# Attention and token mixer in one kernel: x transposed two column blocks ahead of the q products, v transposed one q tile later

## The chip, the cores and the metric

The kernel runs on one core of a Trainium2 chip. Its time is the device time of one execution in microseconds (us); the median of several executions is compared. The engines are TensorE (PE in the profile; PEld is its weight load), VectorE (DVE), ScalarE (ACT), GpSimd (POOL) and SyncE (SP), which issues most DMAs.

## What is computed

x is 2048 tokens by 640 channels. Attention has 32 heads of 20 channels, which share one k and one v; beside it stands a mixer that works across tokens; a gate per token blends the two.

```python
g = _sigmoid((x * gate_w).sum(-1, keepdims=True))
a = _A_ref(x, A_wq, A_wk, A_wv, A_wo)      # q = x@wq, k = x@wk, v = x@wv, softmax(q k^T * 20**-0.5) v, then @ wo
b = _B_ref(x, B_w1, B_b1, B_w2, B_b2)      # LayerNorm, then w1, gelu, w2 across the tokens
return g * a + (1 - g) * b
```

## The kernel before

All instructions are issued by hand in the order that the program writes (a manual schedule), and each engine works through its own list in that order. A step further back in one engine's list never passes an earlier one that waits.

The kernel has a first stage of about 97 us, which is the one that the change touches, and then the mixer's first product (w1), the attention with the rest of the mixer woven in, and a tail. The first stage makes q, k, v, the gate and the layer norm from x. It goes over four **token blocks** of 512 tokens (the loop over `sb`). Products are done in two parts, high and low, of x and of the weights: `wq_hi`, `wq_lo`, and for x the tiles `th`, `tl` (`slot` and `xT_hi`, `xT_lo` in the profile).

For a token block, x must be transposed first. `transpose_x(sb, cs)` transposes column blocks of 128 channels: four 128x128 transposes on TensorE (L292) per column block, into a PSUM bank from the pool `pst` (named `pt`, four banks) for column blocks 0 to 3, and from `psa` (named `pp`, four banks) for block 4. `split_x` then makes the high part on ScalarE (L285) and the low part on VectorE (L286).

The first token block is special, since all its data still has to arrive. SP issues, in turn, column block c of x (256 KB, L195) and rows c of the first three fifths of wq (192 KB, L197). `first_block` works by column block c: `turn(c)` casts wq's rows on GpSimd (`wq_hi`, L370), transposes x and splits it; `first_q(c, j, ahead)` does the products of the three q tiles `ahead` with part j of x (three products, L364); `wq_low` subtracts on GpSimd (L360). Before, the order on TensorE is: six products of a constant tile (L189), transposes of column block 0, two more products of the constant (L377), products 0 high, transposes 1, products 0 low, transposes 2, products 1, transposes 3, products 2, transposes 4, products 3, products 4. The constant products go to a bank that nothing reads.

Then every token block does the following. `project` makes k, v and the gate's logit in one product `pk` (L300, with `wkv_s`, whose low half GpSimd makes at L225); `split_kv` takes it out (L322 on ScalarE, L323 on VectorE, k_hi on ScalarE at L326, k_lo on GpSimd at L327). For each of the five q tiles `m`: transposes of the next token block (from `m` = 2 on: column blocks 0 and 1, then 2 and 3, then 4), the products of tile `m` (L300), `split_q` of the tile before (qh on ScalarE at L315, ql on VectorE at L316, two stores). `turn_v` transposes v and the gate's logit: it takes one bank of `pst`, does four small transposes on TensorE (L340) and two copies on VectorE, `v_sb` (L342) and `z_col` (L343). Between the tiles stand pieces of the layer norm, a generator `norm` that is moved on by `next`: statistics (L233, L234), a power on GpSimd (L242, between L241 and L244), the four small VectorE steps L244 to L247 that give `rstd`, the scaling `ht` (L252), and its split (L265 on ScalarE, L266 on GpSimd). In token block 0 the piece that follows q tile 0 holds L244 to L247, the first L252 and the first L265.

A tile from a pool takes the place of an earlier one, and its first writer waits until the readers of that one are done.

Of the kernel before, what the change touches and what calls it, by code (L numbers as in the profile page):

```python
# [17 lines left out]
P = 128  # L18
S, D, H, DH, F = 2048, 640, 32, 20, 1728
NS = S // P  # L20
DC = D // P
# [3 lines left out]
NB = 512  # L25
# [16 lines left out]
def mix_kernel(ctx: ExitStack, tc: tile.TileContext, A_x, A_wq, A_wk, A_wv, A_wo,  # L42
               B_x, B_w1, B_b1, B_w2, B_b2, gate_w, out):
    nc = tc.nc
# [17 lines left out]
    kst = const.tile([P, S], F32R, name="kst")  # L62
# [110 lines left out]
    with tc.tile_pool(name="pa", bufs=1) as pa, \  # L173
# [9 lines left out]
        def load_x(sb):  # L183
            for st in range(4 * sb, 4 * sb + 4):
                nc.sync.dma_start(out=xts[st], in_=x[st * P:(st + 1) * P, :])

        warm = psa.tile([P, NB], F32, name="pp")
# [32 lines left out]
        def split_wkv():  # L220
            for j in range(2):
                hi = wkv_s[:, :, 32 * j:32 * j + DH + j]
                lo = wkv_s[:, :, 64 + 32 * j:64 + 32 * j + DH + j]
                nc.scalar.activation(hi, wkv[:, :, j, :DH + j], AF.Copy)
                nc.gpsimd.tensor_sub(lo, wkv[:, :, j, :DH + j], f32(hi))  # L225
# [57 lines left out]
        def split_x(sb, c, pt):  # L283
            th, tl = x_tiles(sb, c)
            nc.scalar.activation(th, pt, AF.Copy)  # L285
            nc.vector.tensor_sub(tl, pt, f32(th))  # L286

        def transpose_x(sb, cs):
            pts = [(pst if c < 4 else psa).tile([P, NB], F32, name="pt" if c < 4 else "pp") for c in cs]
            for i in range(4):  # L290
                for c, pt in zip(cs, pts):
                    nc.tensor.transpose(pt[:, i * P:(i + 1) * P], xts[4 * sb + i][:, c * P:(c + 1) * P], ident)  # L292
            return [(sb, c, pt) for c, pt in zip(cs, pts)]

        def project(steps, pp=None, more=False):
            first = pp is None
            if first:
                pp = psa.tile([P, NB], F32, name="pp")
            for n, (w, t) in enumerate(steps):
                nc.tensor.matmul(pp, w, t, start=first and n == 0, stop=not more and n == len(steps) - 1)  # L300
            return pp

        def q_parts(m, ts):
            cols = slice(m * P, (m + 1) * P)
            return [[(wq_hi[:, c, cols], ts[c][0]) for c in range(DC)],
                    [(wq_hi[:, c, cols], ts[c][1]) for c in range(DC)],
                    [(wq_lo[:, c, cols], ts[c][0]) for c in (0, 3, 1, 4, 2)]]

        def split_q(sb, m, pp):
            if (sb, m) == (NQB - 1, DC - 1):  # L310
                qh, ql = (xin[0][:, i, :NB].bitcast(F32R) for i in range(2))
            else:
                qh = paw.tile([P, NB], F32R, name="qh")
                ql = paw.tile([P, NB], F32R, name="ql")
            nc.scalar.activation(qh, pp, AF.Copy)  # L315
            nc.vector.tensor_sub(ql, pp, f32(qh))  # L316
            for j, t in enumerate((qh, ql)):
                nc.sync.dma_start(out=q_scr[j, m * P:(m + 1) * P, sb * NB:(sb + 1) * NB], in_=f32(t))

        def split_kv(pp):  # L320
            kv = pa.tile([64, NB], F32, name="kv")
            nc.scalar.activation(kv, pp[64:, :], AF.Copy)  # L322
            nc.vector.tensor_add(kv, kv, pp[:64, :])  # L323
            k_hi = pa.tile([DH, NB], F32R, name="k_hi")
            k_lo = pa.tile([DH, NB], F32R, name="k_lo")
            nc.scalar.activation(k_hi, kv[:DH, :], AF.Copy)  # L326
            nc.gpsimd.tensor_sub(k_lo, kv[:DH, :], f32(k_hi))  # L327
            return kv, k_hi, k_lo

        def store_k(sb, k_hi, k_lo):  # L330
            cols = slice(sb * NB, (sb + 1) * NB)
            for b in range(2):
                for j, t in enumerate((k_hi, k_hi, k_lo)):
                    o = 64 * b + DH * j
                    nc.sync.dma_start(out=f32(kst[o:o + DH, cols]), in_=f32(t))
# [23 lines left out]
        def wq_low(c, cols, raw):  # L359
            nc.gpsimd.tensor_sub(wq_lo[:, c, cols], raw, f32(wq_hi[:, c, cols]))  # L360

        def first_q(c, j, ahead):
            for m, pp in enumerate(ahead):
                nc.tensor.matmul(pp, wq_hi[:, c, m * P:(m + 1) * P], xT[0, c][j], start=c == 0 and j == 0, stop=False)  # L364

        def first_block():
            ahead = [psa.tile([P, NB], F32, name="pp") for _ in range(QW // P)]

            def turn(c):
                nc.gpsimd.tensor_copy(wq_hi[:, c, :QW], wqs[c])  # L370
                split_x(*transpose_x(0, (c,))[0])

            turn(0)
            for c in range(DC):
                if c == 0:
                    for i in range(2):
                        nc.tensor.matmul(warm, kst[:, :P], kst[:, :NB], start=True, stop=True)  # L377
                    first_q(c, 0, ahead)
                if c + 1 < DC:
                    turn(c + 1)  # L380
                for j in range(c == 0, 2):
                    first_q(c, j, ahead)
                wq_low(c, slice(0, QW), wqs[c])
            load_x(1)
            split_wkv()
            for c in range(DC):
                nc.scalar.activation(wq_hi[:, c, QW:], wqs2[c], AF.Copy)
            for c in (0, 3, 1, 4, 2):
                wq_low(c, slice(QW, D), wqs2[c])
            norm = layer_norm(0)  # L390
            for _ in range(3):
                next(norm)
            return ahead, norm

        due = None
        for sb in range(NQB):
            ahead, norm = first_block() if sb == 0 else ([], layer_norm(sb))
            ts = [xT[sb, c] for c in range(DC)]
            pk = project([(wkv_s[:, c, :], t) for c in range(DC) for t in ts[c]])
            if due:  # L400
                split_q(*due)
            kv, k_hi, k_lo = split_kv(pk)
            if 0 < sb < NQB - 1:
                load_x(sb + 1)
            store_k(sb, k_hi, k_lo)
            if sb:
                next(norm)
            for m in range(DC):
                turned = []
                if sb + 1 < NQB and m > 1 and (sb, m) != (2, DC - 1):  # L410
                    turned = transpose_x(sb + 1, ((0, 1), (2, 3), (4,))[m - 2])
                p = q_parts(m, ts)
                if m < len(ahead):
                    pp = project(p[2], ahead[m])
                elif m < DC - 1:
                    pp = project(p[0] + p[1] + p[2])
                else:
                    pp = project([p[r][c] for c in range(DC) for r in range(3)])
                if m:
                    split_q(*due)  # L420
                due = sb, m, pp
                if m == 0:
                    turn_v(sb, kv)
                for t in turned:
                    split_x(*t)
                if sb == 1 and m == 1:
                    turn_bias()
                if sb == 1 and m == 0:
                    w1_load(3)
                if sb == 2 and 0 < m < 4:  # L430
                    w1_upto(m)
                if sb == 3 and m == 1:
                    w1_upto(4)
                    new_qmax(0)
                if sb == 3 and m == 3:
                    gates()
                for _ in range(1 + (sb and m > 1 or sb == 3)):
                    next(norm, None)
            if sb == 2:
                for t in transpose_x(3, (4,)):  # L440
                    split_x(*t)
# [92 lines left out]
    chain, ahead = [], []  # L534
# [68 lines left out]
    with tc.tile_pool(name="psl", bufs=4, space=PSUM) as psl, \  # L603
# [9 lines left out]
        for fc in range(PRO):  # L613
            pu = [psb.tile([P, NB], F32, name=f"pu{r}") for r in range(2)]
            for hf in range(4):
# [4 lines left out]
                for c in range(HS):  # L620
                    st = hf * HS + c
                    for k, (w, h) in enumerate(((wh, h_hi[0]), (wh, h_lo[0]), (wl, h_hi[0]))):
                        for r in range(2):
                            rows = slice(64 * r, 64 * r + 64)
                            nc.tensor.matmul(pu[r][:, :HD2], w[rows, c, :], h[rows, st, :],  # L625
                                             start=(st == 0 and k == 0), stop=(st == NS - 1 and k == 2))
# [410 lines left out]
    m = len(ph)  # L1037
# [213 lines left out]
    def turn(a, cut):  # L1251
        blocks, cols = slice(a * NB // 64, (a + 1) * NB // 64), slice(a * NB // 2, (a + 1) * NB // 2)
        flat = ot[:, blocks].rearrange("p c e -> p (c e)")
        nc.vector.transpose(flat, o[:, cols])
        nc.vector.reciprocal(rl[:, blocks], ot[:, blocks, DH])
        if cut is not None:
            low(cut)
        nc.vector.tensor_mul(ot[:, blocks], ot[:, blocks], rl[:, blocks, None].to_broadcast([P, NB // 64, 32]))
        nc.vector.transpose(on[:, cols], flat)
        nc.scalar.activation(oh[:, cols], on[:, cols], AF.Copy)  # L1260
# [61 lines left out]
```

## Time and profile before

| | us |
|---|---|
| median of 3 runs | 1618.52 (1618.24 to 1618.57) |
| profiled execution | 1618.09 |
| its span, first to last instruction | 1616.3 |
| TensorE busy in the span | 1609.4 |
| VectorE, ScalarE, GpSimd busy | 1353.7, 1309.0, 868.7 |

A row of the profile's timeline gives the start and the duration in us, the engine, the line of the kernel, the operation, what it writes and reads, the shapes and how often; in square brackets is the idle time of the engine before it and what ended that. Rows that are alike and follow each other are merged. A row of the list of waits gives who waited for whom: us in total, times, the longest. Matmuls overlap in the pipeline, so the distance from one start to the next tells what one costs TensorE.

### The profile page before, as it was taken

The page shows a single profiled execution, that of the slowest core. Times are in us where ns is not written, and L with a number is a line of the kernel's source. Part 1 is how long each engine was busy: PE and PEld are TensorE (multiplying, and loading weights), DVE is VectorE, ACT ScalarE, POOL GpSimd, SP SyncE. Part 2 cuts the span into 40 slices and gives each one's busy share as a digit, 9 for nine tenths or more (in the row PEclk, how much of TensorE's full clock was granted, in tenths as well). Part 3 has the DMA queues.
Part 4 walks back from the last instruction along what each step waited for, and adds up shares of the span by engine and source line. Part 5 has one row for each costly group of instructions (what it writes and reads, how often), then busy time and mean ns, then how long its engine had stood idle before and what let it go on. Part 6 is the DMA issues. An engine that isn't in the chain of part 4 may idle for free.

```text
span 1616.3 us, 39559 instructions
## 1 busy us (share of the span) xinstructions
PE 1609.4 (100%) x14877; PEld 1125.7 (70%) x14877; DVE 1353.7 (84%) x2344; ACT 1309.0 (81%) x2567; POOL 868.7 (54%) x974
## 2 busy tenths in 40 slices
PE   9999999999999999999999999999999999999999
PEld 7889677777777777666666666666666666666666
DVE  6689999999999999888888888888888888666643
ACT  4545788888888888888888888888888888999975
POOL 6568667786777687644544444454544443344410
PEclk9999999999999999999999999999999999999999
DMA  7655223323332232222222221222222212336521
GB/s 216 211 162 150 72 69 79 87 69 93 81 85 71 82 83 65 65 73 81 72 69 73 54 72 55 66 73 81 73 73 69 68 46 70 94 107 192 160 69 45
DMA packets 188245, 144.51 MB, mean 89 GB/s; under 512 B 43473, under 2 KB 150126, under 8 KB 188054
## 3 DMA queue, kind: packets, MB, share of 16 engines
q1 hardware_dynamic: 187766, 141.66, 31.4%
q8 instruction: 117, 1.92, 0.5%
q14 instruction: 74, 0.61, 0.1%
q10 hardware_dynamic: 288, 0.33, 0.1%
HBM read 108.38 MB, written 32.15 MB: 87 GB/s over the span
## 4 chain that ended last, share of the span: by engine, by line
PE 98%; SPq 1%; DVE 0%; ACT 0%; DMA 0%; issue 0%; DVEq 0%; ACTq 0%
PE ms L739 16%; PE g L817 11%; PE s L739 10%; PE ms L704 10%; PE g L1005 9%; PE s L704 8%; PE s L492 6%; PE ms L492 6%; PE pp L300 4%; PE o L739 4%; PE pu L625 3%; PE o L704 3%; PE o L492 2%; PE g L950 2%; PE s L905 1%; PE ml L492 1%
## 5 line engine op out<-in xcount | busy, mean ns | idle before, releaser
L498 DVE TENSOR_REDUCE mp<-s 128x1 f32<-128x512 f32 x878 | 576.8, 681 | 54.5 <-PE s L492 46.2
L713 ACT ACTIVATE p<-ms 128x512 f32<-128x512 f32 x935 | 544.2, 615 | 49.5 <-PE s L739 16.3
L498 DVE TENSOR_REDUCE mp<-ms 128x1 f32<-128x512 f32 x775 | 511.5, 681 | 78.8 <-PE ms L492 64.8
L713 ACT ACTIVATE p<-s 128x512 f32<-128x512 f32 x833 | 488.1, 617 | 34.1 <-PE ms L739 10.7
L752 POOL TENSOR_TENSOR acc<-acc,part 128x512 f32<-128x512 f32 x212 | 274.5, 1295 | 443.2 <-ACT part L751 425.7
L704 PE MATMUL ms<-qst,kst 62*128 62x512 f32 x935 | 366.4, 408 | 0.1
L492 PE MATMUL s<-kst,qmx 60*128 60x512 f32 x878 | 350.8, 414 | 0.6 <-DVE yo L548 0.5
L704 PE MATMUL s<-qst,kst 62*128 62x512 f32 x833 | 323.9, 409 | 0.2 <-ACT p L713 0.2
L492 PE MATMUL ms<-kst,qmx 60*128 60x512 f32 x775 | 307.4, 411 | 0.0
L1005 PE MATMUL g<-slot,wh 64*128 64x320 f32 x1344 | 305.9, 312 | 0.0
L739 PE MATMUL ms<-p,v_sb 128*32 128x512 f32 x2208 | 265.5, 598 | 0.0
L1005 PEld LDWEIGHTS g<-slot,wh 64*128 64x128 f32 x1344 | 216.6, 184 | 68.7 <-issue 55.3
L498 DVE TENSOR_REDUCE mp<-o 128x1 f32<-128x512 f32 x301 | 205.2, 682 | 47.2 <-PE o L492 40.6
L131 POOL TENSOR_TENSOR wl<-wr,wh 128x512 fp32r<-128x512 f32 (+1 forms) x176 | 218.0, 1238 | 29.4 <-ACT wh L128 12.5
L704 PEld LDWEIGHTS ms<-qst,kst 62*128 62x128 f32 x935 | 171.0, 185 | 63.1 <-ACT p L713 23.9
L1005 PE MATMUL g<-slot,wl 64*128 64x320 f32 x672 | 205.2, 305 | 0.0
L817 PE MATMUL g<-slot,wh 64*128 64x320 f32 x864 | 196.3, 309 | 0.0
L817 PE MATMUL g<-u,wh 64*128 64x320 f32 x864 | 196.3, 309 | 0.0
L704 PEld LDWEIGHTS s<-qst,kst 62*128 62x128 f32 x833 | 153.2, 185 | 45.9 <-ACT p L713 29.8
L713 ACT ACTIVATE p<-o 128x512 f32<-128x512 f32 x267 | 164.5, 616 | 11.1 <-PE ms L739 5.5
L739 PE MATMUL s<-p,v_sb 128*32 128x512 f32 x1392 | 167.4, 598 | 0.2 <-ACT p L713 0.2
L492 PEld LDWEIGHTS s<-kst,qmx 60*128 60x128 f32 x878 | 161.4, 185 | 5.0 <-DVE yo L548 0.7
(243 smaller groups left out, 3093.7 us busy)
## 6 DMA issues: line engine op xcount, KB each, us to landing
wr<-in_B_w_dram SPq DMA_DIRECT2D x136, 256.0 KB
qmx<-q_scr SPq DMA_DIRECT2D x192, 80.0 KB
qst<-q_scr SPq DMA_DIRECT2D x192, 80.0 KB
ot<-l_scr SPq DMA_DIRECT2D x120, 64.0 KB
y_scr<-yo SPq DMA_DIRECT2D x16, 320.0 KB
slot<-o_scr SPq DMA_DIRECT2D x16, 320.0 KB
o_scr<-ot SPq DMA_DIRECT2D x124, 40.0 KB
o_scr<-acc SPq DMA_DIRECT2D x124, 40.0 KB
```

Of the source, the lines that this page charges most:

```text
L131: nc.gpsimd.tensor_sub(wl[:, :nv], wr[:, :nv], f32(wh[:, :nv]))
L300: nc.tensor.matmul(pp, w, t, start=first and n == 0, stop=not more and n == len(steps) - 1)
L492: nc.tensor.matmul(ms, qmax[n][64 * b:64 * b + 60, pr, qt * P:(qt + 1) * P], kst[64 * b:64 * b + 60, kq * NB:(kq + 1) * NB], start=True, s ...
L498: r = nc.vector.tensor_reduce(mtiles[n][:, c, kq:kq + 1], ms, axis=AX.X, op=ALU.max)
L625: nc.tensor.matmul(pu[r][:, :HD2], w[rows, c, :], h[rows, st, :], start=(st == 0 and k == 0), stop=(st == NS - 1 and k == 2))
L704: nc.tensor.matmul(s, kst[64 * b:64 * b + 62, kb * P:(kb + 1) * P], q[64 * b:64 * b + 62, pr, :], start=True, stop=True)
L713: e = nc.scalar.activation(p, s, AF.Exp, scale=SCALE)
L739: nc.tensor.matmul(o[32 * hh:32 * hh + 32, :], v_sb[:, kb + i, :], ptiles.pop((u, hh)), start=opened and i == 0, stop=(i == len(us) - 1) a ...
L752: nc.gpsimd.tensor_add(sums[0], sums[0], part)
L817: other_tile(half, nc.tensor.matmul(hold["p"][:, :HD2], w[r, i, :], u[d][r, fc, :], start=(hold["n"] == 1), stop=(hold["n"] == 6 * FC - 3)))
L950: other_tile(half, nc.tensor.matmul(hold["p"][:, :HD2], o[r, c, :], w[r, c, d * HD2:(d + 1) * HD2], start=(hold["n"] == 1), stop=(hold["n" ...
L1005: other_tile(half, nc.tensor.matmul(hold["p"][:, :HD2], w[r, st % HS, :], h[d][r, st, :], start=(hold["n"] == 1), stop=(hold["n"] == 6 * NS)))
```

## The change

In the first token block column block 1 is turned (cast, transposed, split) before the first products, and in the loop column block c + 2 instead of c + 1. The two constant products are gone. In every token block `turn_v` is called after the products of q tile 1 instead of those of q tile 0, so its transposes stand on TensorE behind tile 1's products, and its copies stand on VectorE behind the ql of tile 0.

```diff
             turn(0)
+            turn(1)
+            first_q(0, 0, ahead)
             for c in range(DC):
-                if c == 0:
-                    for i in range(2):
-                        nc.tensor.matmul(warm, kst[:, :P], kst[:, :NB], start=True, stop=True)
-                    first_q(c, 0, ahead)
-                if c + 1 < DC:
-                    turn(c + 1)
+                if c + 2 < DC:
+                    turn(c + 2)
                 for j in range(c == 0, 2):
                     first_q(c, j, ahead)
                 wq_low(c, slice(0, QW), wqs[c])
...
-                if m == 0:
+                if m == 1:
                     turn_v(sb, kv)
```

## The prediction

> **What bounds the kernel now.** I read the chain of waits on the page first, then TensorE's waits, then the first 42 us engine by engine, because the diff touches nothing later: with buffer numbers left out, every engine's order after the four token blocks is the same in both programs.
>
> ```profile
> span 1616.3 us, 39559 instructions
> ...
> PE 98%; SPq 1%; DVE 0%; ACT 0%; DMA 0%; issue 0%; DVEq 0%; ACTq 0%
> ```
>
> TensorE holds 98% of the chain that ended last, so a stretch in which it stands still early is added to the end one for one. All its recorded waits together are small; these two lie in the code that is changed:
>
> ```profile
> PE pp L364 <- ACT slot L285: 0.3, 1, 0.3
> PE pt L340 <- DVE kv L323: 0.2, 1, 0.2
> ```
>
> So there is at most half a microsecond to win at these two places, and the question is what the new order makes TensorE wait for. Its own rows in time (start, duration, engine, line, what, count):
>
> ```profile
> 1.43 2.93 PE L189 MATMUL pp<-kst 128*128 128x512 f32 x6 [1.43 <-DVE kst L68]
> 4.16 1.05 PE L292 MATMUL pt<-ident,xa 128*128 128x128 f32 x4
> 4.87 0.82 PE L377 MATMUL pp<-kst 128*128 128x512 f32 x2
> 5.99 0.94 PE L364 MATMUL pp<-slot,wq_hi 128*128 128x512 f32 x3 [0.31 <-ACT slot L285]
> 6.78 0.60 PE L292 MATMUL pt<-ident,xa 128*128 128x128 f32 x4
> 7.13 0.96 PE L364 MATMUL pp<-slot,wq_hi 128*128 128x512 f32 x3
> ...
> 14.09 0.86 PE L364 MATMUL pp<-xT_lo,wq_hi 128*128 128x512 f32 x3
> 14.78 2.03 PE L300 MATMUL pp<-slot,wkv_s 128*128 128x512 f32 x8
> ...
> 22.34 1.03 PE L292 MATMUL pt<-ident,xb 128*128 128x128 f32 x8
> 23.14 1.17 PE L300 MATMUL pp<-slot,wq_hi 128*128 128x512 f32 x4
> ```
>
> Four transposes of a column block take 0.35 us of TensorE (6.78 to 7.13), three q products 0.79 after a pause (5.99 to 6.78) and 0.69 in a run (14.09 to 14.78, 0.23 each), eight transposes 0.80 (22.34 to 23.14). The k/v product starts at 14.78.
>
> **Part 1: transposes of x two blocks ahead.** They read x column block c+1, and whether it has landed is told by the queue. x and wq blocks alternate on SP's queue, and GpSimd waits for wq's:
>
> ```profile
> 6.96 0.51 POOL L370 CAST wq_hi<-xb 128x384 fp32r<-128x384 f32 x1 [2.26 <-DMA xb<-in_A_wq_dram]
> 7.43 1.03 POOL L360 TENSOR_TENSOR wq_lo<-xb,wq_hi 128x384 fp32r<-128x384 f32 x1
> 8.44 0.50 POOL L370 CAST wq_hi<-xb 128x384 fp32r<-128x384 f32 x1
> ...
> 13.73 0.76 POOL L225 TENSOR_TENSOR wkv_s<-wkv,wkv_s 128x100 fp32r<-128x100 f32 x2
> 14.43 3.54 POOL L360 TENSOR_TENSOR wq_lo<-wr,wq_hi 128x256 fp32r<-128x256 f32 x5
> 18.08 1.04 POOL L242 TENSOR_TENSOR r<-ve,mhalf 128x4 f32<-128x4 f32 x1
> 19.37 1.28 POOL L327 TENSOR_TENSOR k_lo<-kv,k_hi 20x512 fp32r<-20x512 f32 x1 [0.24 <-ACT k_hi L326]
> ```
>
> wq block 1 lands at 6.96. Sizes, and the rate in these microseconds (the last column is GB/s):
>
> ```profile
> xa<-in_A_x_dram SPq DMA_DIRECT2D x5, 256.0 KB
> xb<-in_A_wq_dram SPq DMA_DIRECT2D x4, 192.0 KB
> ```
> ```profile
> 6.00:7.00 1.00, 1.00 (x6) 0.81 (x7) 0.57 (x1) 0.00 (x0) 0.04 (x1) 1.00 1.04 326
> 7.00:8.00 1.00, 1.00 (x8) 0.81 (x7) 0.00 (x0) 0.59 (x1) 1.00 (x2) 1.00 0.94 303
> 8.00:9.00 1.00, 1.00 (x8) 0.92 (x7) 0.69 (x1) 0.45 (x2) 1.00 (x3) 1.00 1.12 368
> ```
>
> The DMA engines are saturated (share 0.94 to 1.12), so landings follow the bytes. Estimates from these rows: x block 1 came 192 KB before wq block 1, at 326 GB/s 0.60 us, so at 6.4; x block 2 behind it at 6.96 + 262/303 = 7.8; wq block 2 at 7.8 + 197/303 = 8.45, which agrees with the cast at 8.44; x block 3 at 8.45 + 262/368 = 9.2.
>
> Now the new order. On TensorE the transposes of block 1 stand in front of the first q products. Those ran from 5.99, in the very time in which block 1 was still on its way; now they wait behind it to 6.4 + 0.35 = 6.75. Next: products to 7.55, transposes of block 2 from 7.8 (waiting) to 8.2, low products to 9.0, transposes of block 3 from 9.2 (waiting) to 9.55. By then twelve transposes (blocks 1 to 3) and six products are done; the old order had done the same twelve and twelve products by about 10.05 (7.13 + 0.79 + 0.35 + 6 x 0.23 + 0.35). Six more products are 1.4, so it stands at 10.95 where it stood at 10.05: **0.9 us late**.
>
> GpSimd is late too, by itself. turn(c) puts the cast of wq block c ahead of the low part of the block before. The old order computed the low part of block 0 (7.43 to 8.44) while block 2 of wq was arriving; the new one waits for block 2, casts it at 8.44, and the low part comes after. GpSimd is busy without a gap from there, so everything behind shifts by one low part, 1.0 us: the low half of wkv_s ends at 15.5 instead of 14.49, the power at L242 runs from 19.0 to 20.05. The k/v product needs wkv_s, so both roads put it at about 15.6, **0.8 late**. The two constant products removed (4.87 to 5.69) stood in idle time: nothing gained, since TensorE is idle to 6.4 now. SP's queue keeps its order, and the one load that waits for GpSimd's low parts, load_x(1), stays where it is:
>
> ```profile
> 14.25 1.77 SPq L185 DMA_DIRECT2D xb<-in_A_x_dram  x4
> ```
>
> The low parts of blocks 0 to 3 that it needs end one part later than before, at about 13.7, still ahead of this issue.
>
> **Part 2: the transposes of v one q tile later.** The step turn_v holds four transposes on TensorE and two copies on VectorE, no DMA. In block 0 the transposes no longer wait for kv. But the copies move on VectorE's queue too, behind ql of q tile 0:
>
> ```profile
> 19.21 0.24 DVE L342 COPY v_sb<-pt 128x80 f32<-128x80 f32 x1 [0.58 <-POOL r L242]
> 19.36 0.15 DVE L343 COPY z_col<-pt 128x4 f32<-128x4 f32 x1
> 19.43 1.24 DVE L244 TENSOR_TENSOR r<-r 128x4 f32<-128x4 f32 x1
> ...
> 21.31 1.13 DVE L252 TENSOR_SCALAR ht<-xa,mv,rstd 128x640 f32<-128x640 f32 x2
> 23.44 0.69 DVE L316 TENSOR_TENSOR ql<-pp,qh 128x512 fp32r<-128x512 f32 x1 [1.00 <-ACT qh L315]
> ```
>
> And somebody waits for them: v's four transposes take one of the four pst banks, and at q tile 3 the second of the two transpose tiles (x blocks 2 and 3, TensorE at 22.34) takes the same bank; in the built program its first transpose waits for the z_col copy. Copies at 19.5 were no obstacle. Copies behind ql, which ends at 24.13, are one: that ql is late because ACT's queue holds the layer norm's casts ahead of qh, and these wait for ht at 21.31, the end of the rstd steps L244 to L247.
>
> When does this chain run in the new kernel? L244 took 1.24 us beside k_lo on GpSimd (19.37 to 20.65) and ended with it: one of them waits for the other. [...] The same happens again: the power ends at 20.05, k_lo starts 4.6 to 4.8 us after the k/v product did (19.37 - 14.78), at 20.3, and holds to 21.6; the rstd steps need 0.6 to 0.8 and are caught. ht then starts at 21.9 to 22.2, I take 22.1, 0.8 later than before; ql ends at 24.13 + 0.8 = 24.9; the copies end 0.3 later (19.21 to 19.51), 25.25; the transposes go on at 25.3, with seven of eight left (0.7), and q tile 3's products start at 26.0 instead of 23.14: **2.9 us late**. TensorE itself would be there at 22.34 + 0.8 - 0.2 (the wait for kv, gone) = 22.95, so 2.3 of it is a new wait, and it swallows the 0.8 of part 1 and the gain on kv. What queues behind the waiting transpose is all of TensorE; VectorE's ql of tile 1, 0.3 us of copies later than otherwise, frees a bank that is wanted at tile 4, fifteen products (3.5 us) after tile 3 begins, and costs nothing.
>
> In blocks 1 to 3 the bank that v takes is not wanted until long after the copies; there the move only puts v's transposes beside others:
>
> ```profile
> 36.19 0.39 PE L300 MATMUL pp<-slot,wq_lo 128*128 128x512 f32 x1
> 36.51 0.42 PE L340 MATMUL pt<-ident,kv 21*128 21x21 f32 x4
> 36.86 1.20 PE L300 MATMUL pp<-slot,wq_hi 128*128 128x512 f32 x4
> ```
>
> Four of them take 0.35 (36.51 to 36.86), and the change of kind costs 0.1 before (36.19 + 0.23 to 36.51) and about 0.1 after. One pair of changes goes in block 1, about one change in block 2, none in block 3: -0.25, bounds 0 and -0.5.
>
> **Sum.** +2.9 - 0.25 = **+2.65 us**, +0.16%. Against the profiled execution (1618.09 us, span 1616.3) that is 1620.75; it lies 0.4 under the median of 1618.52, so the prediction is **1621.2**. A measurement of this kernel can tell about 0.2%, 3.24 us, from no change: the forecast is a loss just inside it. Each of the eight terms is read to 0.1 or 0.2, so the sum is good to about 0.6, and the bound is one such step away.
>
> **Rivals.**
> *The rstd steps escape.* If k_lo starts 0.6 us later against the power than I have it (at 20.9), all four steps are done before it, ht starts at 20.9, and the copies end at 24.0: products at 24.8, +1.7 - 0.25 = +1.4, 1619.9. A TensorE later in part 1 than reckoned does that. Against it: both shift by nearly the same. 0.10, within the bound.
> *No new wait at tile 3.* If the bank is free by 22.95, part 1 and the gains nearly cancel, 0.8 - 0.2 - 0.25 = +0.35, 1618.9; and if x block 1 is there when the first transposes end (4.87), part 1 goes as well and 0.45 us is won: the change then does what its order suggests, and still within the bound. Against it: ql ended at 24.13 even before. 0.09.
> *The copies are held.* They ran while GpSimd was idle; now they run beside its subtractions, and may be held as L244 was, up to 1.1 each: +0.9 to +1.8 more, 1622.1 to 1623.0. Against it: ql at 23.44 has the same source kind (PSUM) and took 0.69. [...] 0.09.
> *TensorE stays slow* (slower side, clear). The first constant products go one in 0.45 us (1.43 to 4.16 for six), later ones in 0.23, while the profile's column of the granted clock says 1.00 throughout: TensorE starts at half speed and is released by 5.99. Two products of the busy stretch before that go, and TensorE idles from 4.87 to 6.4. If the release slips by a few microseconds, the wait at tile 3 hides it, since that wait is set by GpSimd and VectorE; it decides from about 15 us on, and half speed from there to 20 us would add 2.5 more, 1623.7. [...] 0.06.
>
> **How the numbers follow.** My case has 0.64, of which 0.18 lies above the bound (over 3.24) and 0.46 within. Slower by over 0.2%: 0.18 + 0.09 (held copies) + 0.06 (slow TensorE) = 0.33. Within: 0.46 + 0.10 (escape) + 0.09 (no wait) = 0.65. No case gives a gain over the bound; 0.02 is left for something after the four blocks that I don't see. The range leaves out the case without a wait (0.09), that 0.02 and a long slow start (0.06): from 1619.4, under the escape, to 1623.0, the held copies.
>
> **What would show it.** In the profile after: TensorE's second transposes (L292) at about 6.4 and the first q products after, at 6.75; a gap before the casts of wq block 2 on POOL; wkv product near 15.6; L342 and L343 right after the first L316; a wait of about 2.3 us of TensorE on L343 at 22.9, and tile 3's products at 26. Wrong if the L292 pair at tile 3 runs without waiting, if the first products still start at 6.0, or if the change goes past 100 us.

## The result and the profile after

| | before | after |
|---|---|---|
| median, us | 1618.24 (22 runs, 1617.83 to 1618.82) | 1621.15 (22 runs, 1619.57 to 1622.13) |
| profiled execution, us | 1618.09 | 1620.42 |
| its span, us | 1616.3 | 1618.6 |

The ratio is 1.0017, with an interval of 1.0012 to 1.0023: 2.9 us slower, just inside the 0.2% that the prediction took for the bound of what can be told apart; the interval reaches a little beyond it. The times of after spread over 2.6 us, those of before over 1.0.

The engines in the chain that ended last, from the page of after:

```profile
PE 99%; ACT 0%; DVE 0%; DMA 0%; issue 0%; SPq 0%; DVEq 0%; ACTq 0%
```

TensorE still carries the whole chain, so what it loses early arrives at the end. Its waits in the changed code (us in total, times, longest):

```profile
PE pt L292 <- DVE z_col L343: 1.3, 1, 1.3
PE pt L292 <- DMA xa<-in_A_x_dram: 1.0, 1, 1.0
```

Neither is in the list of before. The first is the bank of v at q tile 3, the second x column block 1, which is still on its way. The timeline of TensorE in after:

```profile
6.17 1.12 PE L292 MATMUL pt<-ident,xa 128*128 128x128 f32 x4 [0.96 <-DMA xa<-in_A_x_dram]
6.94 1.63 PE L364 MATMUL pp<-slot,wq_hi 128*128 128x512 f32 x3
8.37 1.05 PE L292 MATMUL pt<-ident,xa 128*128 128x128 f32 x4
9.07 1.41 PE L364 MATMUL pp<-slot,wq_hi 128*128 128x512 f32 x3
10.32 0.60 PE L292 MATMUL pt<-ident,xa 128*128 128x128 f32 x4
...
16.74 2.03 PE L300 MATMUL pp<-slot,wkv_s 128*128 128x512 f32 x8
...
23.92 0.27 PE L292 MATMUL pt<-ident,xb 128*128 128x128 f32 x1
25.51 0.95 PE L292 MATMUL pt<-ident,xb 128*128 128x128 f32 x7 [1.32 <-DVE z_col L343]
26.22 1.17 PE L300 MATMUL pp<-slot,wq_hi 128*128 128x512 f32 x4
```

Three products took 1.43 us (6.94 to 8.37) and then 1.25 (9.07 to 10.32), 0.48 and 0.42 each, where before had 0.26: in this execution TensorE came off its half speed only at 10.1 (10.11 on the clock's record). So the k/v product is 1.96 late (16.74 against 14.78). At q tile 3 one transpose of eight goes through at 23.92 and the next waits for the bank; tile 3's products are 3.08 late (26.22 against 23.14). GpSimd and VectorE in the same execution:

```profile
8.32 0.51 POOL L370 CAST wq_hi<-xb 128x384 fp32r<-128x384 f32 x1 [1.15 <-DMA xb<-in_A_wq_dram]
...
18.96 1.04 POOL L242 TENSOR_TENSOR r<-ve,mhalf 128x4 f32<-128x4 f32 x1
21.33 1.26 POOL L327 TENSOR_TENSOR k_lo<-kv,k_hi 20x512 fp32r<-20x512 f32 x1 [1.32 <-ACT k_hi L326]
23.52 5.28 POOL L266 TENSOR_TENSOR slot<-ht,slot 128x320 fp32r<-128x320 f32 x6 [0.94 <-ACT slot L265]
```
```profile
19.91 0.68 DVE L323 TENSOR_TENSOR kv<-kv,pp 64x512 f32<-64x512 f32 x1 [1.02 <-ACT kv L322]
20.51 0.15 DVE L244 TENSOR_TENSOR r<-r 128x4 f32<-128x4 f32 x1
...
21.29 2.17 DVE L252 TENSOR_SCALAR ht<-xa,mv,rstd 128x640 f32<-128x640 f32 x2
24.46 0.69 DVE L316 TENSOR_TENSOR ql<-pp,qh 128x512 fp32r<-128x512 f32 x1 [1.00 <-ACT qh L315]
25.07 0.23 DVE L342 COPY v_sb<-pt 128x80 f32<-128x80 f32 x1
25.22 0.15 DVE L343 COPY z_col<-pt 128x4 f32<-128x4 f32 x1
```

GpSimd waits for wq block 2 (1.15) before the cast at 8.32, and its power at L242 is 0.9 later than before. On VectorE the copies stand right behind ql, and the waiting transpose starts 0.14 after the second has ended. The mixer's first product starts 2.59 late (98.81 against 96.22), so the later token blocks gave back 0.49 of the 3.08. From there to the end the shift falls by 0.2 more.

### The profile page after: what moved, and what is told of

Its sections match the earlier page's. It is cut to its first block, busy times and chain, and to the rows that moved or that the text cites. A ratio compares the mean times of both kernels' runs of the same rounds, so it can differ in the third digit from the quotient of the medians.

```text
span 1618.6 us, 39555 instructions
## 1 busy us (share of the span) xinstructions
PE 1610.1 (99%) x14875; PEld 1126.9 (70%) x14875; DVE 1352.4 (84%) x2344; ACT 1308.7 (81%) x2567; POOL 869.0 (54%) x974
## 4 chain that ended last, share of the span: by engine, by line
PE 99%; ACT 0%; DVE 0%; DMA 0%; issue 0%; SPq 0%; DVEq 0%; ACTq 0%
PE ms L737 16%; PE g L815 11%; PE s L737 10%; PE ms L702 10%; PE g L1003 9%; PE s L702 8%; PE s L490 6%; PE ms L490 6%; PE pp L300 4%; PE o L737 4%; PE pu L623 3%; PE o L702 3%; PE o L490 2%; PE g L948 2%; PE s L903 1%; PE ml L490 1%
```

## Experiments

Each kernel was run in turns with before (medians 1618.37 us in the first set, 1618.44 in the second and third).

**The two parts alone.** `e1_v_only` is before with only the move of v's transposes:

```diff
-                if m == 0:
+                if m == 1:
                     turn_v(sb, kv)
```

> Only part 2 of the change: turn_v after q tile 1, the first block as before. Theory A (the wait of q tile 3's transposes on v's copies sets the loss): k_lo runs at 19.4 as before and holds the layer norm's chain to 20.65, ql of tile 0 ends near 23.5, the copies at 23.85, TensorE arrives at 21.9 and waits 2.0 us; products of tile 3 at 24.6 against 23.14, less 0.5 saved in later blocks: +1.0 us, 1619.2. Theory B (the loss is the late first block alone, v's move is harmless): the kv wait and the later savings are won, -0.5 to -0.9, 1617.5.

Measured: 1619.55 (11 runs), ratio 1.0009 (1.0000 to 1.0018), +1.2, near theory A. Nine runs lie from 1619.32 to 1619.80, two at 1620.95 and 1621.09. TensorE in its profile:

```profile
24.34 0.95 PE L292 MATMUL pt<-ident,xb 128*128 128x128 f32 x7 [1.63 <-DVE z_col L343]
```

The wait for the bank is there with the first block's x order as before, so it belongs to part 2 alone.

`e2_x_only` is after with `turn_v` back at `m == 0`:

```diff
-                if m == 1:
+                if m == 0:
                     turn_v(sb, kv)
```

> Only part 1: transposes of x two blocks ahead and no constant products, turn_v after q tile 0 as before. Theory A: the k/v product starts about 2 us late (16.7 in the profile after, 14.78 before), nothing waits at q tile 3, no later saving: +2.0 us, 1620.2; so the two parts do not add up, part 1 being hidden under part 2's wait in the full change. Theory B: the whole loss and the later saving that is missing here, +2.9 to +3.1, 1621.2.

Measured: 1619.2, ratio 1.0006 (0.9997 to 1.0015), +0.8. Both theories put it too high: the late release from half speed seen above isn't in the profiled execution (1619.48). Two of the eleven runs, at 1620.57 and 1620.73, lie 1.4 to 1.5 above the median; no trace shows why. TensorE was at full speed from 4.5 on, without the constants:

```profile
7.12 0.95 PE L364 MATMUL pp<-slot,wq_hi 128*128 128x512 f32 x3
...
15.69 2.03 PE L300 MATMUL pp<-slot,wkv_s 128*128 128x512 f32 x8
```

The k/v product is 0.9 late, and there is no wait at q tile 3. By the medians the parts give +1.2 and +0.8; together they cost 2.9. The runs below bear on the rest, 0.9.

**The constant products.** `e3_constants_kept` is after with them put back between the two turns, `e4_no_constants` is before without them:

```diff
# e3, against after
             turn(0)
+            for i in range(2):
+                nc.tensor.matmul(warm, kst[:, :P], kst[:, :NB], start=True, stop=True)
             turn(1)
# e4, against before
                 if c == 0:
-                    for i in range(2):
-                        nc.tensor.matmul(warm, kst[:, :P], kst[:, :NB], start=True, stop=True)
                     first_q(c, 0, ahead)
```

> The changed kernel with the two constant products kept, between the transposes of column blocks 0 and 1. Clock theory (TensorE is released from half speed late when these products go): first q products 0.23 apart as before, k/v product at 15.6, ql of tile 0 some 0.7 earlier than in the changed kernel, 1620.2, and executions within 1 us of each other where the changed kernel spreads over 2.6. Rival (arrival of x block 1 alone makes the first block late): k/v product at 16.7, 1621.1, the spread unchanged.

> The kernel before without the two constant products, nothing else. Clock theory: TensorE stays at half speed to about 10 us as in the changed kernel; the twelve products and eight transposes that ran by then are up to twice as long: +1 to +2 us, 1619.3 to 1620.3, with a spread of 1 us or more. Rival (the products stood in idle time and cost nothing either way): 1618.2 to 1618.5, spread as before.

Measured: e3 1621.74, ratio 1.0018 (1.0009 to 1.0027), no better than after, and in two groups: three runs from 1620.1 to 1620.4, eight from 1621.4 to 1622.2. e4 1618.55, ratio 1.0006 (0.9997 to 1.0015), also in two groups: six from 1618.0 to 1618.6, five from 1620.2 to 1620.8. Neither theory had e3's upper group. By its median e4 is at the rival's time, but five of its runs are at the clock theory's or above it. Both profiles were of the lower group, so one more execution of each kernel was profiled.

> The same kernel as e4_no_constants, one more execution seen by the profiler: its times fell into two groups, 1618.0 to 1618.6 and 1620.2 to 1620.8. [...] Rival B: the groups differ in a transfer's landing, and the release comes before 7.5 us in both.

> The same kernel as e3_constants_kept, one more execution seen by the profiler: its times fell into two groups, 1620.1 to 1620.4 and 1621.4 to 1622.2, and the profile showed one of the lower. Theory A (the groups differ by when TensorE comes off its half speed): an execution of the upper group shows the products of the first block at 0.47 us each until 9 to 10 us, one of the lower group at 0.32 before 7. Rival B (the groups differ in a transfer's landing): the upper group has products of 0.32 us before 7 us and a wait for a DMA of over 1 us somewhere before 30.

e4b fell into the upper group, at 1620.76. Its TensorE:

```profile
6.00 1.62 PE L364 MATMUL pp<-slot,wq_hi 128*128 128x512 f32 x3 [0.78 <-ACT slot L285]
...
8.12 1.63 PE L364 MATMUL pp<-slot,wq_hi 128*128 128x512 f32 x3
...
17.14 2.03 PE L300 MATMUL pp<-slot,wkv_s 128*128 128x512 f32 x8
```

Three products take 1.4 us (6.00 to 7.41) to beyond 10 us, and the k/v product is at 17.14, 2.35 later than in e4's first profile (14.79), which had the same order and an early release (three products in 0.77 us from 6.00). So without the constants the release can come late: here it came at 11.06, not before 7.5 us as rival B had it. If the whole upper group comes of that, which this one trace doesn't show, it costs before's order some 2.1 us in five runs of eleven; before itself showed no such group in any of its runs.

e3b fell into its upper group too, at 1621.47, but not by that. It was released early (k/v product at 15.25, ahead of the lower group's 15.68). What it has is this, behind the wait at q tile 3:

```profile
24.80 0.96 PE L292 MATMUL pt<-ident,xb 128*128 128x128 f32 x7 [2.08 <-DVE z_col L343]
25.51 1.96 PE L300 MATMUL pp<-slot,wq_hi 128*128 128x512 f32 x4
27.27 0.63 PE L300 MATMUL pp<-xT_hi,wq_hi 128*128 128x512 f32 x1
27.70 1.71 PE L300 MATMUL pp<-slot,wq_hi 128*128 128x512 f32 x4
```

Nine products take 3.73 us (25.51 to 29.24) where they need some 2.1. TensorE fell back to half speed (the granted clock is 0.50 from 26 to 29 us). Neither theory of e3b had this: A's half speed was right, its place was not.

**Two more executions of the changed kernel.**

> The changed kernel unaltered, one more execution seen by the profiler. Theory A (its times from 1619.6 to 1622.1 differ by where TensorE's stretches of half speed lie): an execution of 1621.2 or more shows, besides or instead of a release at 10 us, a second stretch of half speed of 3.4 us within the first 40 us; one of 1620.6 or less shows none. Rival B (they differ in landings): one release by 10 us and no second stretch in either.

> The changed kernel unaltered, a second such look; the theories expect the same as of e9_after_again.

e9 took 1620.39 and e10 1622.05. In both TensorE was released before 5 us, and waits 2.1 us at q tile 3. TensorE in e9:

```profile
25.17 0.96 PE L292 MATMUL pt<-ident,xb 128*128 128x128 f32 x7 [2.09 <-DVE z_col L343]
```

and in e10, with its windows (stretch in us, its length, TensorE's busy time and instructions, the granted clock, the DMA share, GB/s):

```profile
25.04 1.49 PE L292 MATMUL pt<-ident,xb 128*128 128x128 f32 x7 [2.12 <-DVE z_col L343]
```
```profile
24.00:26.00 2.00, 0.96 (x6) 0.82 0.32 82
26.00:28.00 2.00, 2.00 (x7) 0.50 1.06 337
28.00:30.00 2.00, 2.00 (x9) 0.82 0.47 160
```

The clock is 0.5 for 0.72 + 2.00 + 0.72 = 3.4 us, from 25.3 to 28.7, and the mixer starts 1.46 later in e10 than in e9 (99.92 against 98.46). Theory A holds for both: a second stretch of half speed in the execution above 1621.2, none in the one below 1620.6.

**Taking the wait away.** `e6_v_ahead_of_ql` is after with the copies of v issued ahead of tile 0's ql; TensorE's order stays:

```diff
+                if m == 1:
+                    turn_v(sb, kv)
                 if m:
                     split_q(*due)
                 due = sb, m, pp
-                if m == 1:
-                    turn_v(sb, kv)
```

> The changed kernel, with v's transposes still behind q tile 1's products, but their two copies issued ahead of tile 0's ql. Theory A (tile 3's transposes wait 1.3 us for a bank because the copies stand behind ql on VectorE): the copies come at about 23.5 right behind ht instead of 25.1, the wait at tile 3 falls from 1.3 us to under 0.4, and the time to 1621.1 - 1.1 = 1620.0 (1619.7 to 1620.3). Rival B (the wait is one for x's landing or for TensorE's own late start, and only shows on that copy): the wait stays and the time is 1621.1.

Measured: 1619.33, ratio 1.0004 (0.9996 to 1.0013), 1.8 us faster than after. The wait for z_col is gone from the list; the copies ran at 23.98 and 24.13, and TensorE, 1.7 us late in this execution, did not stop for them. So the wait was the copies' place behind ql. It gained more than A's 1.1, which was taken from the wait of 1.3 in the first profile; e9 and e10 show 2.1 there. Five of its runs, from 1618.55 to 1618.82, lie 1.6 to 1.8 below e9, which has no fall, so the wait alone can give that much; how much of the median's gain is falls that went with it isn't shown. The profiled execution fell back elsewhere, behind its wait for x (1.76 us, to 6.89):

```profile
6.00:8.00 2.00, 1.10 (x7) 1.00 0.97 300
8.00:10.00 2.00, 2.00 (x9) 0.58 1.14 337
10.00:12.00 2.00, 2.00 (x8) 0.56 0.73 94
```

**Filling the wait.** `e8_filled_wait` is e3 with six useless products ahead of q tile 3's transposes, into the bank that is free:

```diff
+            if sb == 1 and cs == (2, 3):
+                for i in range(6):
+                    nc.tensor.matmul(pts[0], wq_hi[:, 0, :P], xT[0, 0][0], start=True, stop=True)
             for i in range(4):
                 for c, pt in zip(cs, pts):
                     nc.tensor.transpose(...)
```

> The kernel of e3_constants_kept with six more products, whose result is overwritten, ahead of q tile 3's transposes in the first block: 6 x 0.23 = 1.4 us of useless work on TensorE inside its wait for the z_col copy (1.8 to 2.1 us there). Theory A (the upper group of e3 is TensorE falling back to half speed for 3.4 us because the wait leaves it idle for over half of such a stretch): the wait falls to 0.4 to 0.7 us, no execution falls back, the group at 1621.4 to 1622.2 is gone and the median is 1620.2 (1619.9 to 1620.6), 1.5 us faster than e3 with more work. Rival B (the groups come of something else, and added work adds time): two groups remain and the median is 1621.7 or above.

Measured: 1620.50, ratio 1.0013 (1.0004 to 1.0022): by the medians 1.2 us faster than e3 with six products more. The two intervals overlap, the runs hardly do: ten of eleven lie from 1620.06 to 1620.76 and the last at 1621.49, where e3 has eight of eleven from 1621.4 on. Its TensorE:

```profile
22.88 1.55 PE L292 MATMUL pt<-slot,wq_hi 128*128 128x512 f32 x6
24.27 0.27 PE L295 MATMUL pt<-ident,xb 128*128 128x128 f32 x1
25.28 0.95 PE L295 MATMUL pt<-ident,xb 128*128 128x128 f32 x7 [0.74 <-DVE z_col L346]
```

The products that nobody reads (here at L292) cost next to nothing in this wait, which VectorE sets (the median is 0.1 to 0.4 above e3's lower group), and the upper group is gone but for one run. Together with the falls in e3b and e10 this makes the fall behind the wait the likely cause of the upper times of e3 and of after; only those two were traced.

**The part that pays.** `e5_v_late_from_block1` is before with v moved in every block but the first:

```diff
-                if m == 0:
+                if m == (sb > 0):
                     turn_v(sb, kv)
```

> The kernel before, with the transposes of v moved behind q tile 1 in every block but the first. Theory A (the move costs only in the first block, where the copies stand behind ql and k_lo; in the later blocks it saves what the changed kernel's trace showed, 0.40 us in block 1 and 0.13 in block 2): 1618.4 - 0.5 = 1617.9, in the bounds 1617.6 to 1618.2. Theory B (the later saving was only slack given back by a late start, as a TensorE that comes later finds its data ready): 1618.4, no change.

Measured: 1617.86 against 1618.44, ratio 0.9997 (0.9988 to 1.0006). By the interval it is not told from no change; by the medians it lies at A, 0.6 lower. TensorE in block 1 shows where it comes from:

```profile
40.18 0.23 PE L340 MATMUL pt<-ident,kv 21*128 21x21 f32 x1
40.19 0.24 PE L347 MATMUL pt<-ident,bb 32*128 32x32 f32 x1
40.26 0.34 PE L340 MATMUL pt<-ident,kv 21*128 21x21 f32 x3
```

v's transposes now stand beside another transpose (L347) and x's, with no product between. From the last product of tile 0 to x's transposes before took 4.53 us (36.19 to 40.72), e5 4.14 (36.39 to 40.53).

## Why the prediction was right, step by step

The forecast was 1621.2 and the median is 1621.15. The mechanism was the one that it gave, but the agreement to 0.05 us is luck: one term was left out, and others were sized too high by about as much. In e9, which has no fall to half speed, +2.74 and -0.50 stand for the sum's +2.9 and -0.25, 0.4 less together, and the median of before is 0.3 under the 1618.52 of the forecast. The median of after lies 0.8 above e9's 1620.39; the likely cause is the term left out, the last one below.

*x block 1, and the first products.* It landed at 6.17 (6.47 and 6.58 in e10 and e9) for 6.4, and the products started at 6.94 (6.88, 6.99) for 6.75. The k/v product was to start at 15.6; it did at 15.62 in e9 and 15.45 in e10, and at 15.69 in e2, the x part alone. GpSimd's power ended at 20.00 for 20.05. So part 1's +0.8 was right, and e2's time is +0.8.

*The constants: nothing gained.* Right for the sum, too simple for the cost. Putting them back into after's order brought nothing (1621.74 against 1621.15); in before's order the release of TensorE can come as late as 11.06 without them (e4b; 5.09 in before), and e4's upper group is missing with them.

*The chain to the copies.* Predicted: rstd steps caught by k_lo, ht at 22.1, ql's end at 24.9, copies to 25.25, transposes at 25.3, products at 26.0. In e9 L245 took 1.25 beside k_lo, ht began at 21.98, ql ended at 24.81, the copies at 25.02, the transposes went on at 25.17 and the products began at 25.88: each step 0.1 to 0.2 early. GpSimd and VectorE in e9:

```profile
20.27 1.26 POOL L327 TENSOR_TENSOR k_lo<-kv,k_hi 20x512 fp32r<-20x512 f32 x1 [0.21 <-ACT k_hi L326]
```
```profile
20.29 1.25 DVE L245 TENSOR_TENSOR r<-r,ve 128x4 f32<-128x4 f32 x1
...
21.98 1.14 DVE L252 TENSOR_SCALAR ht<-xa,mv,rstd 128x640 f32<-128x640 f32 x2
24.12 0.69 DVE L316 TENSOR_TENSOR ql<-pp,qh 128x512 fp32r<-128x512 f32 x1 [1.00 <-ACT qh L315]
24.72 0.23 DVE L342 COPY v_sb<-pt 128x80 f32<-128x80 f32 x1
24.87 0.15 DVE L343 COPY z_col<-pt 128x4 f32<-128x4 f32 x1
```

In the first profile the four rstd steps did escape, since L244 stands behind the kv sum on VectorE's queue (which the prediction had missed) and that and k_lo shift together; but then ht was caught instead (2.17 for the two, 1.13 before), and the copies ended 0.1 later than predicted. That is why the escape, a rival with 0.10, gave nothing: it counted on ht running free beside k_lo, and ht is held in place of the four steps (in e6 too: 2.16 for the two, beside k_lo).

*The new wait of 2.3.* It is 2.1 in e9 and e10, and 1.3 in the first profile, where TensorE came 1 us late.

*TensorE stays slow.* The first profile is this rival's first half, and went as it said: the release at 10.1 made the k/v product 1.1 later than in e9, and the wait at q tile 3 swallowed 0.8 of it (26.22 against 25.88 is 0.34).

*The copies are held.* Refuted: 0.23 and 0.15 us beside GpSimd's subtraction at L266. Before has the same, 0.24 for v_sb with GpSimd idle and 0.15 for z_col at 19.36, which already ran beside k_lo (from 19.37); the prediction had read both as beside an idle GpSimd.

*The later blocks.* Sized at -0.25 with bounds of 0 and -0.5; measured -0.49 (+3.08 at tile 3, +2.59 at the mixer) and -0.50 in e9. The mis-sized part is block 1: there the transposes of v join both x's and one of the biases (L347), and 0.40 goes instead of some 0.2.

*The term that was missing.* A wait of 2 us early in the kernel can cost more than 2 us: in e10 3.4 us at a clock of 0.5 followed it, which added 1.5 to 1.7; in e9 none did. Eleven of after's 22 runs lie at 1621.29 or above, as e10 does. How many of these fell back, the runs without a trace don't tell. It would also explain why e1 and e2 don't add up to after by the medians: e9, without a fall, is 2.0 above the median of before beside it, which is the sum of +1.2 and +0.8, and e1's wait is 1.6, with only two of its eleven runs 1.5 higher.

## What to carry to other kernels

Ask of a moved step not only what it waits for but which bank its tile takes, who wants that bank next, and what stands ahead of its last reader on that reader's queue: two copies of 0.4 us in all, put behind one ql, held all of TensorE for 2 us. Price an early wait of TensorE of some 2 us with the half speed that may follow (1.5 to 1.7 us in e10, nothing in e9), and profile several executions when times come in groups. Where such a wait can't be removed, useless products can fill it: here they made the kernel 1.2 us faster by the medians.

## What was not expected of the hardware

The instants at which TensorE's clock changes differ from one execution to the next, of the same kernel too. The records of the granted clock in these traces give full speed from 4.45 us (e2), 4.81 (e10), 4.92 (e6), 5.09 (before), 5.14 (e3b), 6.31 (e3), 7.00 (e1), 10.11 (after) and 11.06 (e4b), and half speed again from 25.29 to 28.71 (e10), 25.62 to 29.03 (e3b) and 8.34 to 11.75 (e6). Each of these three stretches of half speed is 3.41 us long, and from release to fall e10 and e3b have 20.48 us.

In the 3.41 us ahead of each release TensorE was 88% (3.02 us, e2) to 100% busy by the rows of the timeline, products and transposes together. A busy stretch as such brought no release: in e1 TensorE was busy without a break from 1.44 to the release at 7.00 (5.56 us), in before from 1.43 to 5.09 (3.66 us), and in e4b from 1.43 to 5.22 (3.79 us) with the release only at 11.06.

In the 3.41 us ahead of a fall TensorE was busy for 38% (e10), 39% (e3b) and 48% (e6). But up to the end of e9's wait, at 25.17, it was 39% too (1.32 us), and up to the end of e2's wait for x, at 6.70, 47% (1.61 us), and both kept the clock (1.00 from 20 to 32 us in e9, from 6 to 12 in e2). So an idle share of over half, which theory A of e8 gave as the cause of the falls, does not settle one. The falls stand behind waits of 1.76 us (e6), 2.08 (e3b) and 2.12 (e10); behind e9's wait of 2.09 there is none. What decides a release or a fall isn't shown.

Transposes follow the clock as products do: in the first profile of after four of them take 0.70 us at half speed (8.37 to 9.07) and 0.36 at full speed (10.32 to 10.68).
